# Attention and a routed mixture of experts on one core: order of the turned-row copy and of the split of the maxima

## The chip, the cores and the metric

One NeuronCore of a Trainium2 chip runs the whole program. The metric is the device time of one execution in microseconds (us); the times shown are medians of several runs. TensorE (PE) multiplies, VectorE (DVE), ScalarE (ACT) and GpSimd (POOL) work on elements, SyncE (SP) and ACT start transfers. PEld is the loading of weights into TensorE, which overlaps its matmuls.

## The reference

Two parts, one behind the other. The first is causal attention over 8 batches of 8 heads, 576 positions, head width 64, with a bias made from the running sum of a gate `s`:

```
cum    = cumsum(max(s, 0))
scores = q @ k.T / sqrt(64)  +  min(-(cum[i] - cum[j]), 0)     masked above the diagonal
attn   = softmax(scores);  out = attn @ v
```

The second takes the result as 4608 rows of 512, chooses a group (4) and an expert (4 in each) by the largest logits, and puts every row through its expert, `relu(x @ w1) @ w2`, scaled by the two softmax weights.

## The kernel before, in words

**Stages.** Attention takes the time to about 430 us, the experts the rest. The change touches attention alone. The 64 heads are worked in 32 pairs `p`, one head a step, and a step is given to PE as a list of items of three kinds, which belong to three heads so that PE always has work:

- A, rowmax of head `s+4`: the product `pm` (L220) goes to one of two PSUM banks, and DVE takes its maximum over each row (`mx`, L228, and the instruction behind it that writes the accumulated maximum `mc`). The items differ in width: 64, 192, 320, 448 and 288 twice.
- B, scores of head `s`: the products `ps` (L276, L278) go to a ring of three PSUM banks, and ACT takes the exp into `pt` or `pu` (L286); POOL sets the masked corner to zero (L295).
- C, output of head `s-1`: `po` (L316), and ACT copies the values `vals` (L321) and the sums `sums` (L324).

**Shift rows.** When both heads of a pair have their maxima, PE transposes them (`shift_rows`, product `pmt`, L242) into the one bank of the pool `ps_t`; DVE splits the negated maxima into a high and a low part, `th` (L248) and `tl` (L249); two transfers started by ACT (L254) put them into rows 66 and 67 of the operand `WA`, where the scores of that pair, two pairs of steps later, subtract the maximum inside the product.

**Normalising.** Behind a pair's second sums DVE transposes them (`st`, L344), takes the reciprocal `rc` (L350), transposes back (`st`, L355) and multiplies (`xT`, L363). The result `xT` goes two ways. ACT rounds it (`xTh`, L376 in `high()`) and POOL takes the rest (`xTl`, L380): these feed the router's logits. And PE transposes it (`rows_out`, product `px`, L409, in the `ps_t` bank again) and ACT copies the turned rows (`xr`, L415 in `leave()`), which SP stores.

**Router.** Each batch is four pairs. When its rows are there, a generator works the routing in small steps between the items: logits `lg` (L733, L734, L737, in a bank of the ring), ACT's copy `lT` (L783), a small product `pr` (L787) in the `ps_t` bank, and some thirty short DVE instructions over the following steps. In a batch's first pair (`c == 0`) `high()` makes sure by `rt.read(p // 4)` that the logits of the batch before have been issued, since its buffers are then reused.

**What sets the order.** The order of instructions on PE, DVE, ACT and POOL in attention is written out by hand. `ORDERS` holds two strings, for even and odd steps. A capital with a digit issues an item; a single letter pops the oldest entry of the queue of that name: `a` maxima, `b` exps, `v` values or sums, `e` the masked corner, `T` the transpose of the maxima, `t` their split, `D` their two transfers, `W` the transpose back, `K` the product `xT`, `O` the turning of the rows, `o` the copy `xr`, `X` the rounding `xTh`, `L` the low part, `S`, `G` and `J` input splits and router work, `R` a router step. `keep(k, n)` pops queue `k` until `n` entries are left; `need(k, i)` pops until the entries up to pair or head `i` are out. The bank of `ps_t` is taken through `small()`, which first does `keep("t", 0)` and `keep("o", 0)`. Each engine runs its instructions in the order in which they were issued; SP's order is left to the scheduler.

**Input splits.** ACT rounds the next pair's inputs (`hl`, L158) and POOL forms their low part (L162), for a part of them straight into the operand `WB`.

Of the kernel before, what the change touches and what calls it, by code (L numbers as in the profile page):

```python
# [19 lines left out]
B, H, S, D = 8, 8, 576, 64  # L20
# [33 lines left out]
def attn_moe(ctx, tc, qk, v, s, wr, w1, w2, out, stop_at=None, dbg=None):  # L54
# [23 lines left out]
    st.listed, st.added = {}, {}  # L78

    attention(tc, qk, v, s, wr, xs, st)  # L80
    if dbg is not None:
        nc.sync.dma_start(dbg['x'], xs)
# [20 lines left out]
def behind(tc, later, earlier):  # L103

    tc.add_manual_dep(later.ins, earlier.ins.name, mybir.DependencyInfo(mybir.DependencyClass.NoSync,
                                                                       mybir.DependencyReason.DATA), reason="behind")
# [8 lines left out]
def attention(tc, qk, v, s, wr, xs, st):  # L115
# [3 lines left out]
    with ExitStack() as ctx:  # L119
# [215 lines left out]
        def normalise(p, vals, sums):  # L335

            c = p % 4
            m = {}

            def turn():  # L340
                for k in "YZWK":
                    need(k, p - 1)
                m["f"] = sm.tile([P, S], F32, name=f"st{p}", tag="st", bufs=1)
                nc.vector.transpose(m["f"], sums)  # L344
                push("Z", p, recip)

            def recip():
                f = m["f"]
                rc = m["rc"] = sm.tile([P, S // 32], F32, name=f"rc{p}", tag="rc", bufs=2)
                nc.vector.reciprocal(rc, f.rearrange("p (b c) -> p b c", c=32)[:, :, 0])  # L350

                push("W", p, back)

            def back():
                nc.vector.transpose(m["f"], m["rc"].unsqueeze(2).to_broadcast([P, S // 32, 32]))  # L355
                push("K", p, finish)

            def finish():
                for k in "OXLM":
                    need(k, p - 2)  # L360
                x = m["x"] = sm.tile([P, S], F32, name=f"xT{p}", tag="xT", bufs=2)
                xTs[p] = x
                nc.vector.tensor_tensor(out=x, in0=vals, in1=m["f"], op=ALU.mult)  # L363
                push("X", p, high)
                push("O", p, lambda: rows_out(p))

            def high():
                x = m["x"]
                if c == 0:
                    for k in "LMQ":  # L370
                        need(k, p - 1)
                    rt.read(p // 4)
                    xhl[p // 4] = [late.tile([P, 4, 512], F32R, name=f"xT{n}{p}", tag=f"xT{n}", bufs=1) for n in "hl"]
                    xtail[p // 4] = XT[p // 4 % 2]
                xh, xl = (t[:, c] for t in xhl[p // 4])
                st.xh = nc.scalar.copy(xh, x[:, 0:512])  # L376
                push("L", p, lambda: low(xh, xl, x))

            def low(xh, xl, x):
                st.xl = (nc.gpsimd if p < NP - 2 else nc.vector).tensor_tensor(  # L380
                    out=xl, in0=x[:, 0:512], in1=xh.bitcast(F32), op=ALU.subtract)
                push("M", p, lambda: tail(x))

            def tail(x):
                i = nc.scalar.copy(xtail[p // 4][:, 64 * c:64 * c + 64], x[:, 512:576])
                if p == NP - 1:
                    behind(tc, i, st.xh)
                b = p // 4
                if p == NP - 2:
                    push("Q", p, lambda: rt.logits(b, *xhl[b], range(3)))  # L390
                if c == 3:
                    push("Q", p, lambda: route(b))

            push("Y", p, turn)

        def route(b):
            if b == B - 2:
                rt.queue.append(rt.first())
            if b == B - 1:
                rt.queue.append(rt.start())  # L400
            rt.queue.append(rt.batch(b, xtail.pop(b), *xhl.pop(b)))

        def rows_out(p):

            b, c = p // 4, p % 4
            x = xTs.pop(p)
            ps = small(f"px{p}")
            for t in range(4):
                nc.tensor.transpose(ps[:, t * P:(t + 1) * P], x[:, t * P:(t + 1) * P], ident)  # L409
            push("o", p, lambda: leave(p, b, c, ps))  # L410
# [19 lines left out]
        def push(k, i, f):  # L430
            fifo[k].append((i, f))

        def pop(k):
            if fifo[k]:
                i, f = fifo[k].pop(0)
                done[k].append(i)
                f()
# [6 lines left out]
        def need(k, i):  # L444

            while fifo[k] and fifo[k][0][0] <= i:
                pop(k)
# [77 lines left out]
        for t in VT:  # L525
# [7 lines left out]
        vals, sums, pts = {}, {}, {}  # L533

        ORDERS = [o.split() for i, o in enumerate((
# [4 lines left out]
        FIRST = [o.split() for i, o in enumerate((  # L540
# [7 lines left out]
        for step in range(-LEAD, NH + 5):  # L548
            m, a = step + LEAD, step - 1
# [8 lines left out]
            if 0 <= a < NH:  # L558
                p = a // 2
# [1149 lines left out]
```

## Time and profile before

| | |
|---|---|
| median of 3 runs | 876.82 us (876.02 to 877.51) |
| the profiled execution | 876.57 us |
| its span | 874.8 us, 1.8 us around it |
| PE busy | 840.2 us |
| PEld busy | 774.2 us |
| DVE busy | 718.9 us |
| ACT busy | 615.7 us |
| POOL busy | 603.2 us |

The busy time of an engine is counted over the whole span, and a matmul's end is modelled. Instructions overlap a little at their ends, so one can begin shortly before the end of the one ahead of it as printed. In a timeline a bracket tells how long the engine was idle before an instruction and which instruction released it.

### The profile page before, as it was taken

To read this page: it belongs to the slowest core of one execution; us is meant where nothing else is said; L and a number is where in the kernel's file an instruction comes from. 1 tells how busy PE (TensorE), PEld (TensorE's weight loads), DVE (VectorE), ACT (ScalarE), POOL (GpSimd) and SP (SyncE) were. 2 spreads that over 40 slices of the span, in tenths; PEclk is the share of its full clock that TensorE was granted. 3 is DMA by queue.
4 is the path that set the end of the run, shared out by engine and by line. 5 is a ranking of instruction groups with operands and counts; after the bars stand their busy time and mean duration, and the time that the engine had idled before them with its cause. 6 is when DMAs were issued, how large, how long until landed. Compare 5 with 4: busy or idle time off the path is not lost. (4 is left out here: it accounts for less than half of the span.)

```text
span 874.8 us, 17801 instructions
## 1 busy us (share of the span) xinstructions
PE 840.2 (96%) x5601; PEld 774.2 (89%) x5601; DVE 718.9 (82%) x1975; ACT 615.7 (70%) x1397; POOL 603.2 (69%) x746
## 2 busy tenths in 40 slices
PE   4999999999999999998799999999999999999997
PEld 2788888888888888886689999999999999999996
DVE  7567787787878788787468799999999999999972
ACT  5668777787868777776656656776677767777760
POOL 9767677676877768545657956776777777777660
PEclk9999999999999999999899999999999999999999
DMA  6999898897979898723546655555656565666620
GB/s 189 256 246 253 233 243 225 218 244 195 251 208 241 224 238 209 180 63 121 173 137 216 219 175 202 203 175 187 228 202 195 182 220 198 235 211 223 218 94 26
DMA packets 81877, 174.06 MB, mean 199 GB/s; under 512 B 9676, under 2 KB 45132, under 8 KB 73584
## 3 DMA queue, kind: packets, MB, share of 16 engines
q1 hardware_dynamic: 71664, 152.93, 59.6%
q0 software_dynamic: 7488, 18.89, 5.8%
q10 hardware_dynamic: 2624, 1.03, 0.5%
q8 instruction: 46, 0.75, 0.3%
q14 instruction: 55, 0.45, 0.2%
HBM read 108.97 MB, written 19.69 MB: 147 GB/s over the span
## 5 line engine op out<-in xcount | busy, mean ns | idle before, releaser
L1016 POOL TENSOR_TENSOR wl<-raw,wh 128x512 fp32r<-128x512 f32 x163 | 209.7, 1299 | 82.4 <-ACT wh L1013 58.6
L1013 ACT CAST wh<-raw 128x512 fp32r<-128x512 f32 x256 | 153.9, 616 | 1.8 <-issue 1.8
L228 DVE CUSTOM_DVE_ANT_0 mx<-pm,mask 128x192 bf16<-128x192 f32 (+4 forms) x320 | 127.2, 418 | 31.4 <-PE pm L220 28.7
L1133 PE MATMUL ph<-xh,wh 128*128 128x256 f32 (+13 forms) x512 | 140.3, 300 | 1.8 <-DVE hl L1140 1.8
L220 PE MATMUL pm<-WA 66*128 66x288 f32 (+4 forms) x384 | 123.8, 355 | 15.3 <-DMA WA<-ch 9.5
L276 PE MATMUL ps<-WA 68*128 68x320 f32 (+4 forms) x384 | 135.9, 358 | 2.0 <-DMA WA<-tl 1.9
L1133 PE MATMUL ph<-xl,wh 128*128 128x256 f32 (+13 forms) x512 | 137.8, 301 | 0.0
L316 PE MATMUL po<-pt,VT 128*128 128x256 f32 (+3 forms) x512 | 119.4, 352 | 1.3 <-issue 1.0
L1212 PE MATMUL py<-hh,wh 128*128 128x256 f32 (+13 forms) x448 | 112.9, 302 | 0.0
L1212 PE MATMUL py<-hl,wh 128*128 128x256 f32 (+13 forms) x448 | 112.4, 301 | 0.0
L1139 ACT ACTIVATE hh<-ph 128x256 fp32r<-128x256 f32 (+13 forms) x128 | 53.3, 418 | 83.8 <-PE ph L1133 82.9
L278 PE MATMUL ps<-WB 128*128 128x320 f32 (+4 forms) x384 | 110.7, 301 | 0.0
L1265 DVE STREAM_TRANSPOSE yr<-yT 32x384 f32<-32x384 f32 (+1 forms) x208 | 104.6, 503 | 4.5 <-ACT yT L1209 0.4
L316 PE MATMUL po<-pu,VT 128*128 128x320 f32 (+1 forms) x384 | 105.5, 383 | 1.3 <-POOL pu L295 1.3
L1103 DVE STREAM_TRANSPOSE xt<-xg 32x256 f32<-32x256 f32 (+1 forms) x208 | 102.4, 492 | 2.7
L316 PEld LDWEIGHTS po<-pt,VT 128*128 128x128 f32 x512 | 88.2, 192 | 13.9 <-issue 1.5
L1133 PEld LDWEIGHTS ph<-xh,wh 128*128 128x128 f32 x512 | 95.9, 190 | 2.1 <-DVE hl L1140 1.9
L1133 PEld LDWEIGHTS ph<-xl,wh 128*128 128x128 f32 x512 | 95.2, 190 | 0.2
L162 POOL TENSOR_TENSOR WB<-r,hl 64x576 fp32r<-64x576 f32 x62 | 88.0, 1420 | 6.1 <-DMA WB<-hl 1.8
L1133 PE MATMUL ph<-xh,wl 128*128 128x256 f32 (+13 forms) x512 | 92.0, 299 | 0.0
L220 PEld LDWEIGHTS pm<-WA 66*128 66x128 f32 (+1 forms) x384 | 69.2, 193 | 25.1 <-DVE mc L228 9.8
L380 POOL TENSOR_TENSOR xTl<-xT,xTh 128x512 fp32r<-128x512 f32 x30 | 38.2, 1272 | 76.0 <-ACT xTh L376 55.4
(249 smaller groups left out, 2007.3 us busy)
## 6 DMA issues: line engine op xcount, KB each, us to landing
raw<-in_w_dram SPq DMA_DIRECT2D x64, 1024.0 KB
r<-in_qk_dram SPq DMA_DIRECT2D x32, 576.0 KB
WA<-hl SPq DMA_DIRECT2D x60, 288.0 KB
WB<-hl SPq DMA_DIRECT2D x60, 288.0 KB
VT<-in_v_dram SPq DMA_DIRECT2D x32, 384.0 KB
WB<-hl SPq DMA_DIRECT2D x64, 144.0 KB
xs<-xr SPq DMA_DIRECT2D x15, 512.0 KB
WA<-cumd SPq DMA_DIRECT2D x56, 4.5 KB
```

What stands on the lines that cost most here:

```text
L162: (nc.vector if p < 1 else nc.gpsimd).tensor_tensor(out=hl[:, 2] if part else WB[p % NBB][0:64, KA, h], in0=r[hr, part], in1=hl[hr, part]. ...
L220: nc.tensor.matmul(ps[:rows, :cw], WA[i][0:66, QA, h, QO + q0:QO + q0 + rows], WA[i][0:66, KA, h, QO + c0:QO + c0 + cw], start=True, stop= ...
L228: nc.vector.tensor_tensor_reduce(out=tmp[:rows, :cw], in0=ps[:rows, :cw], in1=mk[:rows], scale=1.0, scalar=-3.0e38 if c0 == 0 else mo, op0 ...
L276: nc.tensor.matmul(ps[:rows, o:o + w], WA[i][0:68, KA, h, QO + k0:QO + k0 + rows], WA[i][0:68, QA, h, QO + q0:QO + q0 + w], start=True, st ...
L278: nc.tensor.matmul(ps[:rows, o:o + w], WB[p % NBB][:, KA, h, k0:k0 + rows], WB[p % NBB][:, QA, h, q0:q0 + w], start=False, stop=True)
L316: nc.tensor.matmul(po[0][:, qa - base:qb - base], VT[p % NVT].rearrange("p t a d -> p (t a d)")[:, (3 * t + 1 + h) * 64:][:, 0:P], x[:, c: ...
L1013: self.casts.append(nc.scalar.copy(h[:, j], raw[:, j]))
L1016: self.low = lows[self.u, i, j] = nc.gpsimd.tensor_tensor(out=l[:, j], in0=raw[:, j], in1=h[:, j].bitcast(F32), op=ALU.subtract)
L1103: V.transpose(dst[:, 0:n, :, j], src[:, 0:n, :, i])
L1133: self.product = nc.tensor.matmul(pss[f][:, :cap], w[f // 4][:, c, (f % 4) * P:(f % 4 + 1) * P], x[:, c, :cap], start=(c == 0 and w is sel ...
L1212: self.product = nc.tensor.matmul(pss[c][:, :cap], w[2 + f // 4][:, f % 4, c * P:(c + 1) * P], x[:, f, :cap], start=(f == 0 and w is self. ...
L1265: V.transpose(dst[:, 0:n, :, i], src[:, 0:n, :, j])
```

## The change

In `high()` the first pair of each batch now pops the queue `o` up to this pair before anything else, so that the copy `xr` is issued ahead of the router steps that `rt.read` forces and of `xTh`. In the even step's string `t`, the split of the maxima, moves from ahead of `C3` to behind `a a A1`, ahead of `W`, and `D`, the two transfers, from behind `J b` to behind `C5`.

```diff
--- before.py
+++ after.py
@@ -367,6 +367,7 @@
             def high():
                 x = m["x"]
                 if c == 0:
+                    need("o", p)
                     for k in "LMQ":
                         need(k, p - 1)
                     rt.read(p // 4)
@@ -533,8 +534,8 @@
         vals, sums, pts = {}, {}, {}
 
         ORDERS = [o.split() for i, o in enumerate((
-            "b S R B0 R v b a A0 B2 v C0 e G a R a B3 T C1 A3 B1 A2 C2 b e t C3 v G C4 B4 J b D v e a a A1 "
-            "W e A4 C5 e C6 b a A5",
+            "b S R B0 R v b a A0 B2 v C0 e G a R a B3 T C1 A3 B1 A2 C2 b e C3 v G C4 B4 J b v e a a A1 "
+            "t W e A4 C5 D e C6 b a A5",
             "C0 B2 A4 B0 A2 S v e O C1 B1 B3 v X o A0 a Y L b J A3 a v a e b C2 b R K e M C3 G e b Q "
             "e C4 v A1 Z B4 a R A5 C5 b C6 t a a"))]
         FIRST = [o.split() for i, o in enumerate((
```

On DVE, in the even step of a middle pair (between `mx_4_0`, the 288 wide maximum, and `st`, the transpose back), before:

```order
L228 ISA mx_4_0_1778,mc_155<-pm_4_0_1768,mask 128x288
L228 ISA mc_155 128x1
L248 TENSOR_SCALAR th_1802<-pmt_1788 10x128
L249 SCALAR_TENSOR_TENSOR tl_1803<-pmt_1788,th_1802 10x128
L228 ISA mx_2_0_1818,mc_155<-pm_2_0_1791,mask 128x320
L228 ISA mc_155 128x1
L228 ISA mx_1_0_1820,mc_155<-pm_1_0_1796,mask 128x192
L228 ISA mc_155 128x1
L355 STREAM_TRANSPOSE st_1688<-rc_1727 128x576
```

and now:

```order
L228 ISA mx_4_0_1778,mc_155<-pm_4_0_1768,mask 128x288
L228 ISA mc_155 128x1
L228 ISA mx_2_0_1812,mc_155<-pm_2_0_1791,mask 128x320
L228 ISA mc_155 128x1
L228 ISA mx_1_0_1814,mc_155<-pm_1_0_1796,mask 128x192
L228 ISA mc_155 128x1
L248 TENSOR_SCALAR th_1818<-pmt_1788 10x128
L249 SCALAR_TENSOR_TENSOR tl_1819<-pmt_1788,th_1818 10x128
L355 STREAM_TRANSPOSE st_1688<-rc_1727 128x576
```

The two instructions `th` and `tl` have moved from ahead of the 320 and the 192 wide maximum to behind both, directly ahead of `st`; the same holds for 28 pairs. Lines behind 370 are one higher in the changed kernel.

On ACT, in the same even step (`DMA` is the start of a transfer, `ps_2_0` the 512 wide scores, `ps_0_256` the 320 wide ones), before:

```order
L286 ACTIVATE pt_118<-ps_2_0_2150 128x512
L254 DMA WA_110<-th_2169 1x10x128
L254 DMA WA_110<-tl_2170 1x10x128
L324 ACTIVATE sums_2029<-po_0_2144 64x256
L286 ACTIVATE pu_119<-ps_0_256_2160 128x320
L286 ACTIVATE pt_118<-ps_4_0_2177 64x64
```

and now:

```order
L286 ACTIVATE pt_118<-ps_2_0_2150 128x512
L324 ACTIVATE sums_2029<-po_0_2144 64x256
L254 DMA WA_110<-th_2185 1x10x128
L254 DMA WA_110<-tl_2186 1x10x128
L286 ACTIVATE pu_119<-ps_0_256_2160 128x320
L286 ACTIVATE pt_118<-ps_4_0_2173 64x64
```

The sums go ahead of the two transfers, which now stand directly ahead of the 320 wide exp.

On ACT, in the first pair of a batch (the odd step; `px` are the turned rows, `lg` the router's logits), before:

```order
L324 ACTIVATE sums_2029<-po_1_2165 64x320
L286 ACTIVATE pt_120<-ps_0_0_2218 128x256
L286 ACTIVATE pu_121<-ps_0_256_2233 128x320
L783 COPY lT<-lg_2252 40x512
L376 CAST xTh_2262<-xT_2205 128x512
L415 COPY xr_2265<-px_2227 128x4x128
L286 ACTIVATE pt_120<-ps_2_0_2237 128x512
L321 COPY vals_2207<-po_0_2209 64x256
```

and now:

```order
L324 ACTIVATE sums_2029<-po_1_2165 64x320
L416 COPY xr_2243<-px_2227 128x4x128
L286 ACTIVATE pt_120<-ps_0_0_2218 128x256
L286 ACTIVATE pu_121<-ps_0_256_2233 128x320
L784 COPY lT<-lg_2254 40x512
L377 CAST xTh_2264<-xT_2205 128x512
L286 ACTIVATE pt_120<-ps_2_0_2237 128x512
L321 COPY vals_2207<-po_0_2209 64x256
```

The copy `xr` has moved from behind `lT` and `xTh` to ahead of two exps. This is so in the first pairs of batches 2 to 7; in those of batches 0 and 1 it has only changed places with `xTh`. PE's and POOL's orders are the same as before. On SP the load of `VT` now goes ahead of one load of `WA` in some pairs.

## Rows read from the trace of the kernel before

**Rows 1.** busy time by stretch, 60 to 390 us: engines in order, clock, DMA
```profile
60.00:390.00 330.00, 327.47 (x2125) 285.20 (x2124) 268.52 (x992) 257.64 (x653) 231.74 (x362) 1.00 0.82 218
```

**Rows 2.** waits, 60 to 390 us, PEld, then DVE: us in all, times, longest
```profile
PEld pm L220 <- DVE mc L228: 2.4, 7, 0.6
PEld pr L787 <- ACT xr L415: 1.6, 5, 0.3
...
DVE th L248 <- PE pmt L242: 8.6, 11, 1.0
```

**Rows 3.** timeline, DVE, router-loaded step: start us, us, instruction, [idle before <-releaser]
```profile
211.02 0.27 DVE L248 TENSOR_SCALAR th<-pmt 10x128 fp32r<-10x128 f32 x1
...
211.53 0.47 DVE L228 CUSTOM_DVE_ANT_0 mx<-pm,mask 128x320 bf16<-128x320 f32 x1
211.94 0.07 DVE L228 DVE_READ_ACCUMULATOR2_ANT mc<- 128x1 f32 x1
...
212.22 0.76 DVE L355 STREAM_TRANSPOSE st<-rc 128x576 f32<-128x576 f32 x1
...
213.22 0.76 DVE L363 TENSOR_TENSOR xT<-vals,st 128x576 f32<-128x576 f32 x1
...
214.44 0.08 DVE L228 DVE_READ_ACCUMULATOR2_ANT mc<- 128x1 f32 x1
```

**Rows 4.** timeline, PE, the same step
```profile
212.06 0.75 PE L220 MATMUL pm<-WA 66*64 66x64 f32 x2 [0.15 <-DVE mc L228]
...
214.71 0.37 PE L220 MATMUL pm<-WA 66*128 66x448 f32 x1
```

**Rows 5.** timeline, DVE, a step without router work
```profile
244.16 0.28 DVE L248 TENSOR_SCALAR th<-pmt 10x128 fp32r<-10x128 f32 x1 [0.63 <-PE pmt L242]
...
245.09 0.34 DVE L228 CUSTOM_DVE_ANT_0 mx<-pm,mask 128x192 bf16<-128x192 f32 x1
...
245.36 0.76 DVE L355 STREAM_TRANSPOSE st<-rc 128x576 f32<-128x576 f32 x1
...
246.49 0.90 DVE L363 TENSOR_TENSOR xT<-vals,st 128x576 f32<-128x576 f32 x1
...
247.86 0.08 DVE L228 DVE_READ_ACCUMULATOR2_ANT mc<- 128x1 f32 x1
```

**Rows 6.** timeline, PE, the same step
```profile
244.65 0.26 PE L220 MATMUL pm<-WA 66*128 66x192 f32 x1
...
248.29 0.37 PE L220 MATMUL pm<-WA 66*128 66x448 f32 x1
```

**Rows 7.** timeline, POOL, the same step
```profile
246.86 1.81 POOL L162 TENSOR_TENSOR WB<-r,hl 64x576 fp32r<-64x576 f32 x1
```

**Rows 8.** timeline, ACT, the router-loaded step
```profile
212.14 0.72 ACTq L254 DMA_DIRECT2D WA<-tl  x1
...
213.31 0.44 ACT L286 ACTIVATE pu<-ps 128x320 f32<-128x320 f32 x1
```

**Rows 9.** timeline, ACT, the step without router work
```profile
248.57 0.54 ACT L286 ACTIVATE pu<-ps 128x448 f32<-128x448 f32 x1 [0.57 <-PE ps L278]
```

**Rows 10.** timeline, ACT, first pair of a batch
```profile
201.17 0.44 ACT L286 ACTIVATE pu<-ps 128x320 f32<-128x320 f32 x1
...
204.89 0.58 ACT L415 COPY xr<-px 128x512 f32<-128x512 f32 x1
205.37 0.59 ACT L286 ACTIVATE pt<-ps 128x512 f32<-128x512 f32 x1
```

**Rows 11.** timeline, PE, the same place
```profile
201.79 0.45 PE L733 MATMUL lg<-xTh,wr_sb 128*40 128x512 f32 x1
...
205.52 0.62 PE L787 MATMUL pr<-xtl,wr_f 128*20 128x64 f32 x8 [0.20 <-ACT xr L415]
```

**Rows 12.** timeline, DVE, another step
```profile
102.71 1.38 DVE L363 TENSOR_TENSOR xT<-vals,st 128x576 f32<-128x576 f32 x1
```

**Rows 13.** timeline, POOL, the same step
```profile
102.07 1.40 POOL L162 TENSOR_TENSOR WB<-r,hl 64x576 fp32r<-64x576 f32 x1
```

## The prediction

> **What bounds the kernel now.** I read the page first, to see which engine could set the end, then a table of one stretch, then the waits of that stretch, and last the timeline engine by engine at the places that the change touches. The page's busy time of TensorE (PE), 840.2 of 874.8 us in the table above, is an average over two stages, so the stretch from 60 to 390 us, which holds only attention and the router steps between, was read by itself: PE is busy 327.47 of 330.00 us there [rows 1]. Whatever the change does to VectorE (DVE), ScalarE (ACT) or GpSimd (POOL) in attention can therefore give back at most 2.5 us of shown PE idle time, or what the weight loads (PEld) ahead of the matmuls were held, which counts a little more. The waits of that stretch say what holds them [rows 2]: seven weight loads for a rowmax product wait for the accumulated maximum `mc` of DVE, 2.4 us in all and 0.6 at most, and five for the router product `pr` wait for the ACT copy `xr`, 1.6 us in all. Those are the two waits that the two parts of the change touch. A third row of that view counts: DVE itself waits for the transposed maxima `pmt` ahead of `th` eleven times, 8.6 us in all, so in these steps `th` and `tl` lie in time that DVE had free.
>
> The yardstick is the profiled execution, 876.57 us, 0.25 below the median of 876.82. A change of 0.2% is 1.75 us, about what a measurement of this kernel can tell from none; so "no change" goes from 875.07 to 878.57.
>
> **Part A: `th` and `tl` behind the wide maxima.** The even step keeps every instruction; on DVE the two small ones move from ahead of the 320 and 192 wide maxima to behind them, ahead of `st`. Nothing is added to any engine. There are two kinds of step to cost.
>
> *Steps loaded with router work* (six between 60 and 390; 209 to 216 us is read here). DVE is behind PE, and from `th` at 211.02 to `mx` at 211.53 are 0.51 us [rows 3]. The 192 wide maximum's `mc` ends at 212.01, and the weight load and matmul of the 64 wide product begin at 212.06, released by it [rows 3, 4]; this also gives 0.05 us as the shortest step from a `mc` to its product. With `th` and `tl` out of the way both maxima come 0.51 earlier and this wait, 0.6 at most, is gone. But `th` and `tl` then stand ahead of `st`, so `st` still begins at 212.22, the product `xT` still at 213.22, and the `mc` behind it still ends at 214.52 [rows 3]. The 448 wide product that opens the odd step needs that `mc`, and it began at 214.71 [rows 4]: 0.19 after, of which 0.05 must stay. So what is late next is this product, and PE keeps 0.14 us of its lead. Six steps: 6 x 0.14 = 0.84 us gained. The bounds: nothing, if some other wait takes the same 0.14; and 2.4 us, the sum of the waits that go, if `xT` were to end earlier.
>
> *Steps without router work* (eleven, by the waits for `pmt`; 242 to 250 us is read here). Before, `th` began at 244.16 after DVE had waited 0.63 for `pmt` [rows 5]. That free time was the cover of `th` and `tl`, and it goes, since DVE takes the maxima first, as soon as PE has them. The product for the 192 wide one ends at 244.65 + 0.26 = 244.91 [rows 6], so its maximum begins at 244.96 instead of 245.09; `th` follows at 245.23 (0.27 behind it, as `st` did before), and `st` at 245.23 + 0.51 = 245.74 instead of 245.36: 0.38 later [rows 5]. Before `xT` some of that is made up: `xT` begins 1.13 after `st` here, but 1.00 after it in the loaded step [rows 3, 5], so it comes 0.25 to 0.38 later. The room behind: `mc` ends at 247.94 and the 448 wide product starts at 248.29 [rows 5, 6], 0.35, less 0.05 that must stay, 0.30. So PE loses between 0 and 0.08 a step, 0 to 0.9 us over eleven. I take 0.2, near the lower end: `xT` lasts 0.90 here against 0.76 in the loaded step, beside a POOL split that begins 0.37 after it [rows 3, 5, 7], and a later `xT` has as much or less of its length ahead of that split's end. The other even steps lie between the two kinds and I cost them at nothing: their maxima come neither 0.51 earlier nor `st` 0.38 later.
>
> *ACT's queue.* The row transfers of `th` and `tl` go out from ACT, 0.72 us of issue each, and in the loaded step the second ends at 212.86, where ACT goes on [rows 8]. These transfers now go behind `sums` and ahead of one exp, which waits for DVE's `tl`. In the loaded step `tl` is done about 0.7 later, in the other 1.07 later, and the exp at 213.31 [rows 8] comes some 0.3 later, in the other kind 0.7. What hides it: ACT then has an idle stretch of 0.57 ahead of the wide exp at 248.57 [rows 9], and the bank that this exp frees is one of three, needed by PE about an exp later. That cover is thin; if it is gone the rest, 0.1 us a step, goes to PE's bank wait, 11 x 0.1 = 1.1 us. I take nothing and keep 1.1 for the range. SyncE's loads change places among themselves only; they lead their use by far more than a transfer's length, and cost nothing.
>
> **Part B: `xr` ahead of `xTh`.** In the first pair of batches 2 to 7 the copy `xr`, 0.48 us of ACT's line (204.89 to the next start at 205.37 [rows 10]), goes from behind `lT` to ahead of two exps; five of these six places have the wait for `pr`, 1.6 us in all [rows 2]. Its early end is a gain only if PE isn't held elsewhere first. The exp that begins at 201.17 and ends at 201.61 [rows 10] frees the bank for the logits `lg`, which began at 201.79 [rows 11]. Moved by 0.48 it ends at 202.09, and with 0.05 on top `lg` starts at 202.14, 0.35 later. All PE work behind moves by 0.35, and the wait for `xr` ahead of `pr` at 205.52, some 0.33 (1.6/5) [rows 2, 11], is gone at the same time. Net: +0.02 a place, 0.1 over five, which I take as 0. Between the ends: -1.6 us if the exps aren't held up, +1.75 (5 x 0.35) if `pr` should wait as long for something else. On ACT `lT` waits for `lg` in both orders, so what is taken out behind it (`xr`) comes out of time that ACT needs for the exp that follows, and PE doesn't wait for that one. POOL's order is unchanged. In batches 0 and 1 `xr` and `xTh` only swap, at nothing.
>
> **The sum.** -0.84 + 0.2 + 0 = -0.6 us. From 876.57 that is 876.0, from the median 876.2; I say 876.1.
>
> **Rivals.** *1. The waits come back whole (faster).* If `pr`'s wait goes and `lg` isn't held, -1.6 - 0.84 + 0.2 = -2.2: 874.3. If the seven waits for `mc` also go in full, -4.0: 872.6. For it: PE's idle time has no larger rows [rows 2]. Against it: `st` and `xT` keep their times in the loaded step, and the exp's end lies only 0.18 ahead of `lg` [rows 10, 11]. Chance 0.22.
>
> *2. POOL takes `xT`'s place (slower).* In the steps without router work `xT` moves from 246.49 to between 246.74 and 246.87, and the POOL split `WB` starts at 246.86 [rows 5, 7]. Once `xT` is the later of the two, it is held: at 102.71 it began 0.64 behind such a split and lasted 1.38 against 0.90 [rows 12, 13]. The point from which it decides is a shift of 0.37, all but the upper end of mine. Begun at 246.86 it would end at 248.24; `mc` ends 0.55 after `xT` ends (247.39 to 247.94), at 248.79, and the product starts at 248.84 instead of 248.29, 0.55 us a step [rows 5, 6]. In half of the eleven steps that is 3.0 us, with the gain of 0.84 taken off +2.2: 878.8; in all eleven 881.8. Against it: the splits start at different points of a step, and in most the shift stops short. Chance 0.15.
> The Trainium skill, SBUF — State Buffer, section "Who interferes with whom", says that a DVE instruction with two SBUF inputs contends with a GpSimd instruction that reads SBUF, and that whoever issues first holds the shared ports for its whole instruction while the other fully blocks. By that rule `xT` at 102.71 would have stood until the split's end at 103.47 and lasted 0.76 + 0.76 = 1.52, and the `xT` at 246.49, being first, 0.76; the trace has 1.38 and 0.90, so it agrees on who loses and not on whole blocking.
>
> *3. Nothing reaches PE (no change).* The loaded steps' 0.14 is taken by the neighbouring wait, and B cancels: 876.6. It shares its sign with my forecast, and the two have 0.63 together, the forecast 0.43 of it.
>
> **How the numbers follow.** Faster by over 1.75 us only with rival 1: 0.22. Slower by over 1.75 only with rival 2 or with the upper ends of ACT and `lg` together: 0.15. Between: 0.63. For eight in ten the range goes down to 874.0, just past the milder form of rival 1, and up to 878.5, which takes in the ends of part A (+0.9), ACT (+1.1) or `lg` (+1.75) but only the edge of rival 2.
>
> **What would show it.** In the changed trace the weight load ahead of the 64 wide product should no longer wait for `mc` in the loaded steps, and a shorter wait for `mc` should stand ahead of the 448 wide product of the odd step instead; the row of `th` waiting for `pmt` should vanish. `pr` should not wait for `xr`, and `lg` should wait for an exp, about 0.35 at five places. I am wrong if `xT`'s mean goes up by some tenths with waits for `mc` of half a microsecond or more (rival 2), if the waits vanish without a successor (rival 1), or if PE waits for an exp behind the row transfers.

## The result and the profile after

The changed kernel took 884.2 us (median of 6 runs, 881.42 to 885.04) against 875.75 for the kernel before (6 runs): a ratio of 1.0095, 95% interval 1.0073 to 1.0117. It is slower by about 8 us, where the prediction had 876.1 and a range up to 878.5. Its profiled execution took 883.62 us with a span of 881.8, 7.0 us more than before; the rows below are read from these two executions.

Where in the span the time went is read from one instruction that both kernels have once a pair, the transpose of the maxima `pmt` on PE. Two rows of the timeline of each kernel, for the transposes of pairs 7 and 31 (start, duration, instruction), the kernel before first:

```profile
100.09 0.27 PE L242 MATMUL pmt<-ident,mc 128*10 128x128 f32 x1
...
390.26 0.27 PE L242 MATMUL pmt<-ident,mc 128*10 128x128 f32 x1
```

and the changed kernel:

```profile
100.52 0.27 PE L242 MATMUL pmt<-ident,mc 128*10 128x128 f32 x1
...
397.29 0.27 PE L242 MATMUL pmt<-ident,mc 128*10 128x128 f32 x1
```

Up to pair 7 the change has cost 0.43 us; between the two rows it takes 296.77 instead of 290.17, 6.60 more; from the last row to the end of the span both take 484.5. So the loss lies in the steady part of attention, and this stretch of 24 pairs, read from one trace a run, is the measure for all runs below. Its PE row of the view by stretch, which answers to [rows 1], hardly shows it:

```profile
60.00:390.00 330.00, 325.25 (x2074) 276.94 (x2072) 267.59 (x967) 251.28 (x636) 228.04 (x355) 1.00 0.81 214
```

PE still looks busy, 325.25 of 330.00 us, but it got through 2074 matmuls instead of 2125, 2.4% fewer, with 0.157 us of busy time for each instead of 0.154. One reason is shown below in part A: a matmul that is released late can count as busy for longer. The waits of the same 330 us, PEld first and then DVE (us in all, times, longest), answer to [rows 2]; the last row is one of before:

```profile
PEld pm L220 <- DVE mc L228: 8.6, 24, 1.1
PEld L887 <- issue: 3.2, 10, 0.6
PEld pmt L242 <- DVE mc L228: 1.6, 4, 0.4
```

```profile
DVE st L344 <- ACT sums L324: 5.4, 17, 1.1
```

```profile
DVE st L344 <- ACT sums L324: 0.3, 1, 0.3
```

The wait of `pr` for `xr` is gone and so is that of `th` for `pmt`, as forecast. But the seven waits for `mc`, 2.4 us, have become 24 with 8.6, the router product `pw` (L887) waits 3.2 instead of 1.0, and DVE, which waited 0.3 us for ACT's sums ahead of `st` before, now does so 17 times for 5.4.

What else makes DVE late is seen in the groups by line between 119 and 392 us (busy us, mean ns): the router's operations with two inputs in SBUF. Before, and then after:

```profile
L363 DVE TENSOR_TENSOR xT<-vals,st 128x576 f32<-128x576 f32 x23 | 19.2, 834 | 0.8
...
L817 DVE TENSOR_TENSOR eq<-logit,lmx 128x100 f32<-128x100 f32 x5 | 4.9, 982 | 0.2
L868 DVE TENSOR_TENSOR col<-hot,u 128x320 bf16<-128x320 bf16 x6 | 2.9, 488 | 0.0
L864 DVE SCALAR_TENSOR_TENSOR pl<-us,pos 128x5 f32<-128x5 f32 x6 | 2.6, 430 | 0.2
...
L824 DVE TENSOR_TENSOR oh<-fx,desc 128x100 f32<-128x100 f32 x5 | 1.3, 258 | 0.0
```

```profile
L363 DVE TENSOR_TENSOR xT<-vals,st 128x576 f32<-128x576 f32 x22 | 17.9, 816 | 0.7
...
L818 DVE TENSOR_TENSOR eq<-logit,lmx 128x100 f32<-128x100 f32 x5 | 6.3, 1265 | 0.2
...
L865 DVE SCALAR_TENSOR_TENSOR pl<-us,pos 128x5 f32<-128x5 f32 x6 | 4.0, 672 | 0.2
L869 DVE TENSOR_TENSOR col<-hot,u 128x320 bf16<-128x320 bf16 x6 | 4.0, 669 | 0.0
L825 DVE TENSOR_TENSOR oh<-fx,desc 128x100 f32<-128x100 f32 x5 | 2.7, 534 | 0.0
```

`eq` has gone from 982 to 1265 ns, `pl` from 430 to 672, `col` from 488 to 669, `oh` from 258 to 534, with the same shapes. `xT`, on which the slower rival was built, has not: 834 and 816.

### The profile page after: what moved, and what is told of

Same layout as the page of the kernel before. It is cut to its first block, busy times and chain, and to the rows that moved or that the text cites. A ratio compares the mean times of both kernels' runs of the same rounds, so it can differ in the third digit from the quotient of the medians.

```text
span 881.8 us, 17799 instructions
## 1 busy us (share of the span) xinstructions
PE 844.6 (96%) x5601; PEld 771.1 (87%) x5601; DVE 723.5 (82%) x1975; ACT 615.6 (70%) x1397; POOL 602.5 (68%) x746
## 5 line engine op out<-in xcount | busy, mean ns | idle before, releaser
L286 ACT ACTIVATE pu<-ps 128x320 f32<-128x320 f32 (+1 forms) x128 | 62.8, 491 | 58.5 <-DVE mc L228 33.8
L162 POOL TENSOR_TENSOR WB<-r,hl 64x576 fp32r<-64x576 f32 x62 | 91.1, 1469 | 5.9 <-ACT hl L158 3.4
```

The source lines that it names most:

```text
L162: (nc.vector if p < 1 else nc.gpsimd).tensor_tensor(out=hl[:, 2] if part else WB[p % NBB][0:64, KA, h], in0=r[hr, part], in1=hl[hr, part]. ...
```

## The experiments

There are four theories; H, D and B stood before the first runs, P was formed on their traces. **H**: part A costs because ACT is held at the row transfers behind the late split. **D**: part A costs because `th` and `tl` lie on DVE's line ahead of `st`. **P**: what makes DVE late is POOL; whatever makes POOL later (ACT's later roundings) lengthens DVE's two-input operations. **B**: the loss is part B's alone. All runs at a glance; the stretch is from the transpose of pair 7 to that of pair 31, the mean of `eq` is that of 119 to 392 us. The two runs that move the transfers alone, e3_send and e10_sp_late, lie 0.26 and 0.12 us from before; a difference of that size is taken as none:

| run | ratio to before (95%) | stretch us | to before | `eq` ns |
|---|---|---|---|---|
| before | | 290.17 | | 982 |
| the change | 1.0095 (1.0073 to 1.0117) | 296.77 | +6.60 | 1265 |
| e1_rows: part A alone | 1.0045 (1.0022 to 1.0069) | 293.67 | +3.50 | 991 |
| e2_copy: part B alone | 1.0043 (1.0023 to 1.0064) | 292.62 | +2.45 | 1266 |
| e3_send: transfers alone | 0.9985 (0.9956 to 1.0013) | 290.43 | +0.26 | 987 |
| e5_rows_sp: A, sent by SyncE | 1.0074 (1.0048 to 1.0100) | 290.46 | +0.29 | 990 |
| e9_rows_sp_late: the same from pair 6 | 1.0009 (0.9985 to 1.0032) | 290.64 | +0.47 | 981 |
| e10_sp_late: before, sent by SyncE | 1.0014 (0.9995 to 1.0032) | 290.29 | +0.12 | 986 |
| e8_pool_late: POOL later by a fill | 1.0028 (1.0006 to 1.0050) | 291.68 | +1.51 | 1238 |
| e7_copy_idle: `xr` in ACT's idle time | 0.9997 (0.9978 to 1.0016) | 290.39 | +0.22 | 1264 |
| e12_split: WB split out of `eq`'s way | 0.9982 (0.9966 to 0.9998) | 288.16 | -2.01 | 263 |
| e11_both: e7 and e12 | 0.9978 (0.9962 to 0.9995) | 287.01 | -3.16 | 263 |
| e13_after_split: the change and e12 | 1.0006 (0.9989 to 1.0024) | 290.75 | +0.58 | 262 |

### The parts one by one

e1_rows is the change without its line in `high()`; e2_copy has that line alone; e3_send keeps `t` where it was and moves `D` alone:

```diff
-... b e t C3 v G C4 B4 J b D v e a a A1 W e A4 C5 e C6 b a A5
+... b e t C3 v G C4 B4 J b v e a a A1 W e A4 C5 D e C6 b a A5
```

Expected of e1_rows: 

> Part A alone (the split of the maxima behind the two wide maxima and its two transfers behind the sums; the copy of the turned rows stays behind the rounding). In the changed kernel the exp behind the two transfers starts 0.6 to 0.7 us later after the transpose of the maxima than before (3.33 against 2.61), in every even step. Theory H (ACT is held): this is where most of the loss of 8 us comes from, so this run is 5 to 8 us slower than before. Theory D (DVE is late by the split itself): also 5 to 8 us slower. Theory B (the early copy holds the router's products on PE): within 1.5 us of before.

Expected of e2_copy: 

> Part B alone (the copy of the turned rows ahead of the rounding in each batch's first pair). Theories H and D: within 2 us of before, with the wait of the router product for the copy gone and a wait of the routing products for an exp in its place, 1 to 3 us in all. Theory B: 5 to 8 us slower.

Expected of e3_send: 

> The two transfers alone moved behind the sums, the split stays ahead of the wide maxima. ACT then has nothing to wait for at the transfers. Theories H, D and B: within 1.5 us of before, the exp behind the transfers about as late after the transpose as before (2.6 us). If the place of the transfers in ACT's queue costs by itself, whatever DVE does: over 3 us slower.

Both parts cost, 3.50 and 2.45 us, together nearly the 6.60 of both: part A less than theories H and D had, part B more than they had and less than B had. No theory had it right that the loss is shared. Moving the transfers alone costs nothing.

**Part B.** PE's rows in the first pair of a batch are what the prediction worked out. Before, and in e2_copy (whose rows stand 2.27 us earlier here):

```profile
250.30 0.59 PE L886 MATMUL pw<-val,rows 128*128 128x192 bf16 x5
...
254.40 0.62 PE L787 MATMUL pr<-xtl,wr_f 128*20 128x64 f32 x8 [0.20 <-ACT xr L415]
```

```profile
248.32 0.57 PE L887 MATMUL pw<-val,rows 128*128 128x192 bf16 x5
...
252.15 0.62 PE L788 MATMUL pr<-xtl,wr_f 128*20 128x64 f32 x8
```

`pw` starts 0.29 later, held by the first exp behind `xr`, which ends at 248.27, and `pr` 0.02 later: the 0.29 is lost and the wait for `xr` won back. But POOL's low part `xTl` follows `xTh`, which follows `lT`, which follows the logits, so POOL and all its splits come 0.3 us later too. In the next even step, the kernel before and then e2_copy, `eq` on DVE and the `WB` split on POOL:

```profile
258.42 0.98 DVE L817 TENSOR_TENSOR eq<-logit,lmx 128x100 f32<-128x100 f32 x1
```

```profile
257.86 1.42 POOL L162 TENSOR_TENSOR WB<-r,hl 64x576 fp32r<-64x576 f32 x1
```

```profile
256.17 1.26 DVE L818 TENSOR_TENSOR eq<-logit,lmx 128x100 f32<-128x100 f32 x1
```

```profile
255.90 1.41 POOL L162 TENSOR_TENSOR WB<-r,hl 64x576 fp32r<-64x576 f32 x1
```

Before, the split ends at 259.28 and `eq` at 259.40. In e2_copy the split ends at 257.31 and `eq` at 257.43. The length of `eq` is the time to the end of POOL's split and 0.12 more, in both. Behind `eq` stand `th`, the maxima and the product that needs `mc`: 0.30 us on PE. The largest single loss, 1.09 of the 2.45 us, is in batch 1, where `xr` and `xTh` only swap and the prediction took nothing. It begins at `eq`: `xTh` is late by 0.70, POOL's splits behind it too, and `eq`, which before met only the end of the split `hl`, meets most of it. The first row is before, the next two are e2_copy:

```profile
109.45 0.36 DVE L817 TENSOR_TENSOR eq<-logit,lmx 128x100 f32<-128x100 f32 x1
```

```profile
105.48 1.04 DVE L818 TENSOR_TENSOR eq<-logit,lmx 128x100 f32<-128x100 f32 x1
```

```profile
105.00 1.41 POOL L162 TENSOR_TENSOR hl<-r,hl 128x576 fp32r<-128x576 f32 x1
```

So DVE comes to `oh` (L825) 0.68 us later. Before, `oh` was done when the next split of POOL began; now it runs into it. In e2_copy, `oh`, the split, and the product that waits (start, us):

```profile
107.55 1.27 DVE L825 TENSOR_TENSOR oh<-fx,desc 128x100 f32<-128x100 f32 x1
```

```profile
107.28 1.41 POOL L162 TENSOR_TENSOR WB<-r,hl 64x576 fp32r<-64x576 f32 x1
```

```profile
109.52 0.35 PE L220 MATMUL pm<-WA 66*128 66x192 f32 x1 [0.82 <-DVE mc L228]
```

`oh` takes 1.27 us (its mean is 0.26 where it begins at the end of a POOL instruction or beside none) and ends 0.13 after the split, and PE stands for 0.82.

**Part A.** In the loaded step e1_rows does first what was forecast. Its rowmax products, and those of before (a group's duration is that of its matmuls):

```profile
260.94 0.75 PE L220 MATMUL pm<-WA 66*64 66x64 f32 x2 [0.15 <-DVE mc L228]
...
262.37 0.54 PE L220 MATMUL pm<-WA 66*128 66x288 f32 x1
...
263.59 0.37 PE L220 MATMUL pm<-WA 66*128 66x448 f32 x1
```

```profile
262.41 0.60 PE L220 MATMUL pm<-WA 66*64 66x64 f32 x2
...
263.93 0.40 PE L220 MATMUL pm<-WA 66*128 66x288 f32 x1
...
265.26 0.47 PE L220 MATMUL pm<-WA 66*128 66x448 f32 x1
```

The transposes of this pair start at 258.61 and 260.40, so the 64 wide product comes 2.01 instead of 2.33 after it, and its group ends 0.47 sooner. The 288 wide one keeps 0.23, and of the 448 wide one's start 0.12 is left. But that product now takes 0.47 instead of 0.37: it begins 0.06 behind the end of its `mc`, together with its weight load, which was ahead of it before, and what follows it is where it was. So the 0.14 that I kept a step is 0. The `mc` in e1_rows:

```profile
265.12 0.08 DVE L228 DVE_READ_ACCUMULATOR2_ANT mc<- 128x1 f32 x1
```

Then ACT, in the same kind of step, in the changed kernel, which has part B too:

```profile
217.22 0.76 ACTq L254 DMA_DIRECT2D WA<-tl  x1
218.08 0.44 ACT L286 ACTIVATE pu<-ps 128x320 f32<-128x320 f32 x1 [2.62 <-DVE xT L363]
...
220.23 0.43 ACT L324 ACTIVATE sums<-po 64x320 f32<-64x320 f32 x1
```

```profile
220.69 0.78 DVE L344 STREAM_TRANSPOSE st<-sums 128x576 f32<-128x576 f32 x1 [0.61 <-ACT sums L324]
...
222.15 0.62 DVE L825 TENSOR_TENSOR oh<-fx,desc 128x100 f32<-128x100 f32 x1
```

```profile
221.38 1.28 POOL L381 TENSOR_TENSOR xTl<-xT,xTh 128x512 fp32r<-128x512 f32 x1 [2.46 <-ACT xTh L377]
```

The exp behind the two transfers starts 4.54 us after the transpose (213.54) instead of 3.58 before (213.31 [rows 8] and 209.73), 0.96 later. In four other loaded steps it is 0.59 to 0.66 later, and in e1_rows 0.34 to 0.38; part B's longer `eq` stands ahead of `th` and adds 0.28. There is hardly any idle time on ACT in this step to take that up, so everything behind is late: the sums, for which `st` waits 0.61, and `xTh`, so POOL's `xTl`, which ends at 222.66; `oh` takes 0.62 and ends at 222.77, 0.11 behind it.

The longer `oh` isn't where PE loses, though. By the transposes of e1_rows, the steps that hold it cost -0.03 to 0.02 us against before (pairs 12 to 13, 16 to 17, 20 to 21, 24 to 25), and the steps behind them 0.33 to 0.45 (13 to 14, 17 to 18, 21 to 22, 25 to 26). There `col` runs into the late `xTl`. In e1_rows, DVE, POOL and PE:

```profile
230.39 0.76 DVE L868 TENSOR_TENSOR col<-hot,u 128x320 bf16<-128x320 bf16 x1
```

```profile
229.53 1.28 POOL L380 TENSOR_TENSOR xTl<-xT,xTh 128x512 fp32r<-128x512 f32 x1 [2.46 <-ACT xTh L376]
```

```profile
234.12 0.28 PE L242 MATMUL pmt<-ident,mc 128*10 128x128 f32 x1 [0.22 <-DVE mc L228]
```

`col` takes 0.76 us instead of 0.49 and ends 0.34 behind `xTl`, and the transpose of pair 18 waits for the maxima behind it, which it did not before.

### Is it ACT's hold, or the split's place on DVE?

The same part A, but SyncE starts the two transfers; in e9_rows_sp_late and e10_sp_late only from pair 6 on, so that the start of the program stays as it was, in the latter with the split in its old place:

```diff
-                    nc.scalar.dma_start(WA[i][r:r + 1, QA]...
+                    (nc.sync if p >= 6 else nc.scalar).dma_start(WA[i][r:r + 1, QA]...
```

Expected of e5_rows_sp: 

> Part A alone, but the two transfers are started by SyncE instead of ACT. DVE has the split in its late place, ACT no longer waits for it. Theory H: ACT gets 1.5 us an even step back, so the loss is gone: within 2 us of before or up to 5 us faster. Theory D: the split still lies between the maxima and the transpose back, so 4 to 8 us slower than before, like the run with part A alone. A risk for both: SyncE's loads queue behind the wait for the split; then PE would show waits for transfers.

Expected of e9_rows_sp_late: 

> Part A alone with its two transfers started by SyncE from pair 6 on and by ACT in the pairs before, so that the start of the program is left as it was. Theory H (part A costs because ACT is held at the transfers behind the late split): between the transposes of pairs 7 and 31 within 1 us of before, and the whole time within 2 us of before. Theory D (the late split costs through DVE itself): 3 to 4 us more than before there, as with part A alone.

Expected of e10_sp_late: 

> The kernel before with the two transfers started by SyncE from pair 6 on; the split stays in its old place. It takes 1.44 us of issue an even step off ACT. Theory H with ACT as a partner of the bound: 0 to 3 us faster than before between the transposes of pairs 7 and 31. If ACT has room anyway in the old order: no difference beyond 0.5 us there. If it is as slow as part A alone, SyncE's queue costs by itself and the run before it in this list can't be read as a test of ACT.

With ACT free the stretch of part A goes from +3.50 to +0.29 and +0.47, and e10_sp_late is at +0.12: theory H holds, and D is worth 0.3 to 0.5 us, near the 0.2 that the prediction had for it in the steps without router work. The lengths of `oh`, `pl` and `col` are those of before again, but for one `col` of 0.75 us in e9_rows_sp_late; the step with that `col` (13 to 14) costs 0.26 us, the three others of its kind -0.02 to -0.01. As a whole e5_rows_sp was 0.74% slower all the same. Its profiled execution is 8.2 us longer than that of before: 5.0 us of it lie ahead of the transpose of pair 5, which came at 80.59 instead of 75.56 (71.6 to 77.7 in the other runs), and 2.9 behind that of pair 31. In the first 80 us SyncE, which also starts the loads, stood 8.8 us ahead of these transfers; that this is what made the start late was not traced further, and the 2.9 us stay open. With the start as before, e9_rows_sp_late is level with before. ACT has room in the old order (e10_sp_late), which is why taking 1.44 us a step off it wins nothing.

### Is it POOL?

e8_pool_late makes nothing late but POOL, by a fill that no other instruction needs:

```diff
+                if c == 0 and 4 < p < NP - 2:
+                    d = sm.tile([P, 256], F32, name=f"dummy{p}", tag="dummy", bufs=1)
+                    nc.gpsimd.memset(d, 0.0)
```

Expected: 

> The kernel before, and POOL alone made later: in the first pair of batches 2 to 7 a fill of 128x256 elements (about 0.3 us by the other fills) goes behind POOL's low part xTl. No order on PE, DVE or ACT changes. Theory P: the POOL splits behind it come 0.3 us later, the DVE operation eq of the next even step goes from 0.98 to about 1.26 us, and between the transposes of pairs 5 and 31 the run takes 1.5 to 2.5 us more than before (six places of 0.3). Rival (POOL's times don't matter to DVE, eq is longer for another reason): eq 0.98 and within 0.5 us of before there.

```profile
257.11 0.31 POOL L384 MEMSET dummy<- 128x256 f32 x1
...
260.07 1.42 POOL L162 TENSOR_TENSOR WB<-r,hl 64x576 fp32r<-64x576 f32 x1
```

```profile
260.37 1.24 DVE L820 TENSOR_TENSOR eq<-logit,lmx 128x100 f32<-128x100 f32 x1
```

The fill took 0.31 us, the split ends at 261.49 and `eq` at 261.61, 0.12 behind it again; the mean of `eq` is 1238 ns, and the stretch takes 1.51 us more. Theory P holds: no order on PE, DVE or ACT was changed, and PE's only wait that grew is the one for `mc` (3.9 instead of 2.4 us between 100 and 392 us), so the delay reaches PE by way of DVE. e7_copy_idle turns it round. It gives part B its gain without its harm, by a call from the router ahead of `lT`, so that `xr` lies where ACT waits for the logits and POOL's times stay:

```diff
+                    rt.hook = lambda: need("o", p)
                     rt.read(p // 4)
...
+        if self.hook:
+            self.hook()
         nc.scalar.copy(lT[:40], lg[:40])
```

Expected: 

> Part B done differently: in the first pairs of batches 2 to 7 the copy xr goes behind the two exps and ahead of lT, where ACT waits 2.3 us for the logits; elsewhere nothing moves. The router product should not wait for the copy any more (1.6 us before), POOL's low part and its input splits stay at their times, and the router operation eq of the next even step stays at 0.98 us. Theory P (part B costs because POOL comes 0.3 us later and DVE's two-input operations wait for POOL's splits): 1 to 2 us faster than before between the transposes of pairs 5 and 31 (314.7 us before). Rival (a copy ahead of the rounding costs by itself): 1 to 3 us slower there, as with part B alone.

```profile
257.85 1.27 DVE L822 TENSOR_TENSOR eq<-logit,lmx 128x100 f32<-128x100 f32 x1
```

```profile
257.57 1.42 POOL L162 TENSOR_TENSOR WB<-r,hl 64x576 fp32r<-64x576 f32 x1
```

This expectation failed: +0.22, not -1 to -2. The wait of `pr` is gone and DVE comes to `eq` 0.28 us sooner against POOL (0.28 behind the start of the split, 0.56 before), but the split ends at 258.99 and `eq` at 259.12. What was won at `pr` was given back there.

The last three runs take POOL out of `eq`'s way. In every fourth even step the first `WB` split goes behind the masked corner of `pu`, which waits for a later exp:

```diff
+            if order is ORDERS and step % 8 == 6:
+                seq = list(seq)
+                seq.remove("G")
+                seq.insert(seq.index("C2") + 3, "G")
```

Expected of e12_split: 

> The kernel before, and in every fourth even step (those with the router operation eq) POOL's first WB split goes behind the masked corner of pu, so that POOL does not hold an input split while DVE has eq to do. Nothing else moves. Theory P: eq goes from 0.98 to between 0.26 and 0.5 us, th and the maxima behind it come up to 0.5 us earlier, the wait for mc ahead of the 64 wide product (six times 0.3 to 0.6) goes, and between the transposes of pairs 7 and 31 the run is 1 to 2.5 us faster than before (290.2 us). If the length of eq has nothing to do with POOL: eq stays at 0.98 and the time is within 0.5 us there. A risk: the second WB split then meets xT and gives some of it back.

Expected of e11_both: 

> The copy xr in ACT's idle time ahead of lT (as in the run before with the copy there) and the WB split out of the way of eq. Theory P: there the 0.3 us a batch that PE won at the router product was lost to eq at 1.26 us; with the split out of the way eq is short and the gain stays: 2 to 4 us faster than before between the transposes of pairs 7 and 31. If the gain is lost to anything else: no better than the run with the split alone.

Expected of e13_after_split: 

> The changed kernel, and the WB split moved as in the two runs above. Theory P: eq goes from 1.26 to under 0.5 us and the changed kernel gets back what part B costs, 2 to 4 us between the transposes of pairs 7 and 31 (296.8 us in the changed kernel); what part A costs through oh, pl and col, in other steps, stays. If it gets back less than 1 us, the lengthened eq was a sign of the delay and not its cause.

The loaded step of e12_split, DVE and then POOL:

```profile
257.48 0.26 DVE L822 TENSOR_TENSOR eq<-logit,lmx 128x100 f32<-128x100 f32 x1
...
260.49 0.97 DVE L363 TENSOR_TENSOR xT<-vals,st 128x576 f32<-128x576 f32 x1
```

```profile
257.68 0.29 POOL L295 TENSOR_SCALAR_AFFINE_SELECT pu<-pu 128x128 f32<-128x128 f32 x1 [0.73 <-ACT pu L286]
257.95 2.90 POOL L162 TENSOR_TENSOR WB<-r,hl 64x576 fp32r<-64x576 f32 x2
```

`eq` takes 0.26 us, and the kernel is faster than before by 2.01 us in the stretch and 0.9982 as a whole (interval just below 1). By the transposes, five steps with `eq` win 0.45 to 0.50 us each, and the one of batch 1, where `eq` was short before, loses 0.33. Some is given back, as expected: `xT` now runs beside the splits and takes 0.97. With `xr` in ACT's idle time as well, e11_both is at -3.16 and 0.9978, 1.4 past the sum of the two (-2.01 and +0.22): the gain at `pr` isn't taken by `eq` any more. By the stretch it is the fastest kernel here; as a whole it can't be told from e12_split. And the changed kernel with the split moved goes from +6.60 to +0.58, level with before; I had expected 2 to 4 us back and got 6.0. `pl`, `col` and `oh` are still long there (600, 667 and 477 ns), so part A isn't mended but paid for: by the transposes each of the five steps with `eq` is now 0.53 to 0.55 us shorter than before, and the steps with a long `col` behind them still cost 0.28 to 0.63. In batch 1 the moved split leaves `oh` alone instead (0.26 us), which is 0.8 of the 6.0.

## Why the prediction was wrong

Two steps failed. In part B it is a sentence that had no number, "POOL's order is unchanged": POOL came 0.3 us later with its order unchanged (0.7 in batch 1), and that cost 2.45 us. In part A it is the one on ACT's queue that took nothing for the exp's delay and looked for harm only in PE's wait for a bank: the delay cost 3.0 to 3.2 us, by way of DVE. Point by point:

- **Loaded steps, -0.84.** The wait for the 64 wide product went, and the 448 wide product was next, as said. Its price was mis-sized: a product that comes just behind its `mc` takes 0.10 us longer by the rows of e1_rows, so nothing of the 0.14 stayed.
- **Steps without router work, +0.2.** The bounds 0 to 0.9 hold: with ACT free, the late split cost 0.3 to 0.5 over the stretch, both kinds of step together.
- **ACT, 0.** The delay was sized right for the steps without router work: 0.71 by the trace (3.32 against 2.61 after the transpose of pair 19). For the loaded step I said "some 0.3"; it was 0.34 to 0.38 in e1_rows and 0.59 to 0.96 in the changed kernel, where the longer `eq` comes on top, and its cover was taken from the other kind of step [rows 9], which has 0.57 us of idle time that the loaded one lacks. With it ACT's roundings, and so POOL, and the sums, and so `st`, are late. This is 3.0 to 3.2 us, the difference between e1_rows and the two runs with SyncE. How much of it goes by POOL and how much by the sums was not tried by itself; the four steps with a long `col` hold 1.6 of the 3.50 us of e1_rows.
- **Part B, 0.** `lg` held for 0.35 against `pr` free by 0.33: measured 0.29 and 0.27. The mechanism and the sizes on PE were right, except that the product held is `pw`, which stands ahead of `lg`, by the exp ahead of the one that I named. What wasn't costed is the 0.3 us by which POOL moved with the logits, some 1.4 of the 2.45 us in the stretch; and the swap in batches 0 and 1, "at nothing", of which batch 1 alone has the other 1.09.
- **Rival 2** named POOL holding a two-input operation of DVE, at 878.8 with a chance of 0.15. It was the right mechanism at the wrong place: it put it at `xT` behind the late split, and it struck `eq`, `oh`, `pl` and `col`, whose rows I hadn't read against POOL's. `xT` is no longer than before.

The rule of the Trainium skill, SBUF — State Buffer, section "Who interferes with whom", that whoever issues first has the shared ports for its whole instruction, fits these rows better than I gave it credit for. Whenever they began inside a subtraction of POOL with over 0.2 us of it to go, `eq` and `oh` end 0.12 us behind its end, `pl` 0.02 to 0.03, and the `xT` of [rows 12, 13], which I took for part-way blocking, 0.62, like every other `xT` that begins so in these traces (0.61 to 0.62). Each of these is the length that the operation has by itself (0.26, 0.17 and 0.76 us), less 0.14. What doesn't fit is [rows 5, 7], where `xT` is first: there both get longer, `xT` 0.90 and POOL's split 1.81 us.

## What to carry to other kernels

An unchanged order on an engine is no price of zero: ask when each of its instructions now starts, and which instructions of other engines run beside it. In these traces a short DVE operation with two SBUF inputs that began inside a subtraction of POOL had no length of its own but ended with it, so gains upstream of it were lost (e7_copy_idle) and most of POOL's delay was paid by PE (0.25 of 0.31 us a batch in e8_pool_late, on average); moving the long POOL instruction won 2 us where moving the waits had lost 8. A lengthened operation isn't a loss yet, either: `oh` in part A cost PE nothing, `col` one step later did. And the cover that hides a delay has to be read in the kind of step where the delay occurs.

## What was not expected of the hardware

- An `eq` of 128x100 elements takes 0.26 us by itself and 0.98 to 1.26 us beside a POOL subtraction of 64x576, ending 0.12 us after it; POOL's own instruction, where it began first, stays at 1.41 us (1.40 to 1.42) whether DVE waits for it or not.
- The wait has one size whatever waits: `eq`, `oh`, `pl` and `xT`, of 0.17 to 0.76 us by themselves, each end their own length less 0.14 us behind the end of the POOL subtraction that they began in, if over 0.2 us of it were to go.
- A 66x448 product released 0.06 us behind its maximum took 0.47 us instead of 0.37, with PE shown as busy; it goes with this that the view by stretch counted PE as 325.25 of 330 us busy while it did 2.4% fewer matmuls (2074 against 2125).
